# The front of an SSM and MLP kernel: a planner's order against a fixed list with idle products in it

## The chip, the cores and the metric

The kernel runs on one core of a Trainium2 chip. The metric is the device time of one execution, in microseconds (us). The kernel before takes 1021.8 us, the median of three runs (1018.9 to 1024.1). Five engines of the core work side by side, each through its own queue in order: TensorE (PE, matrix products, with its weight loads PEld), VectorE (DVE), ScalarE (ACT), GpSimd (POOL) and SyncE (SP), which starts most of the transfers.

## The reference: what is computed

`x` holds 2048 tokens of 640 channels. A vector `c` gives six rows of modulation, a shift, a scale and a gate for each half of the block:

```python
mod = (silu(c) @ w_mod).reshape(1, 6, 1, 640)
sa, ca, ga, sb, cb, gb = mod rows
h = layernorm(x) * (1 + ca) + sa
x = x + ga * S4(h)                # first half
h = layernorm(x) * (1 + cb) + sb
x = x + gb * (silu(h @ w1) * (h @ w3)) @ w2     # second half
```

`S4` convolves each channel over the 2048 tokens with a kernel of its own length. That convolution kernel is `K[d, l] = Re(sum over n of C B dt exp(dt A l))`, with 128 complex states `n` for each channel `d`; the reference convolves by Fourier transforms of twice the length, and adds `h * Dskip`.

## The kernel before, in words

The second half (the MLP, from about 430 us on) is not touched. The first half has these kinds of work, which the change and the prediction speak of by two-letter words:

- **Parameters** (`polar`, L221): from A, B, C and dt to the magnitudes and phases of every state. It runs once for the first 128 channels and once for the other 512. It uses logarithm and arctangent on ACT, and ends in four transposes on PE and in the split operands `lah`, `lal`, `lmh`, `lml`, from which exponentials are made.
- **Modulation** (`mod_early`, `mod_cols`, `mod_shift`, `mod_gate`, L278 to L344): `w_mod` is loaded in pieces of columns. A piece costs ten products of `silu(c)` with it, a copy to SBUF, and small products that turn the row into columns.
- **Token tiles**: 16 tiles of 128 tokens. Each is loaded (`ln1_load`), normed (`ln1_norm`), and sent through the first stage of the transform (`u_stage1`): products on PE, two copies out of PSUM, and a store to DRAM. Seven `x` tiles have room at a time.
- **Generation of the convolution kernel**: 40 steps of 16 channels. A step has phases on POOL (`PH`), absolute value, cosine and sine on ACT (`AB`, `CO`, `SI`), products for the exponents on PE and the exponentials on ACT (`PA`, `XA` and `PQ`, `XQ`), four table products on DVE (`E1`, `E2`, `A1`, `A2`), 64 small products on PE into the PSUM bank `pk` (`kg`), two operations on DVE that read `pk` (`K`), and a first transform stage (`pt` on PE, `uk` on ACT).
- **The convolution itself**: 40 steps, each with a transfer of twiddle factors, products (`st`), a copy (`kc`), products and sums on DVE (`T`, `Y`), inverse products with another transfer (`iv`), and a store (`zt`).

ACT holds one table of functions at a time: one for exponentials, one for sines, one for the logarithm, one for the arctangent. A change of table is an instruction of its own in ACT's queue.

The order is set in two ways. `keep` and `act` (L113 to L119) hold instructions in the order of the program text. Everything else is placed by a planner. Before, ACT is always held in order, and the other engines only once `in_order` is set. The front of the first half, from L702 to the end of the loop `for tk in range(LAG)` at L753, is planned: parameters, modulation and token tiles are written one after the other, with generation steps 0 to 9 in a loop, and the planner mixes them. After it comes a fixed list, `ROUND` (L805). It holds one pass over four generation steps and four convolution steps, in a fixed order on all engines, and is run ten times. What the front has already made is skipped, through the set `done`. So the first passes are short, and the third is the first with convolution steps in it.

Of the kernel before, what the change touches and what calls it, by code (L numbers as in the profile page):

```python
# [9 lines left out]
F32 = mybir.dt.float32  # L10
# [82 lines left out]
def tile_kernel(ctx: ExitStack, tc: tile.TileContext, a):  # L93
# [22 lines left out]

    def act(*args, **kw):

        return tc.keep_in_program_order(S.activation(*args, **kw))  # L119
# [26 lines left out]
    cT = kp.tile([P, KD], F32, name="cT")  # L146
    uk = kp.tile([P, 3, NA, DC], F32, name="uk")
# [18 lines left out]
    scb = pm_.tile([P, KD, NA], F32, name="scb")  # L166
# [3 lines left out]
    lt = pm_.tile([P, 2, D - DC], F32, name="lt")  # L170
    misc = pm_.tile([P, 9 * NA + 1 + P], F32, name="misc")
    selx, stepx = misc[:, :NA], misc[:, NA:4 * NA]
    s1r, c1, one4 = misc[:, 4 * NA:6 * NA], misc[:, 6 * NA:8 * NA], misc[:, 8 * NA:8 * NA + 1]
# [9 lines left out]
    def w_load(w, c0):  # L183

        n = w.shape[2]
        for i in range(c0 // 480, (c0 + n - 1) // 480 + 1):
            lo, hi = max(c0, i * 480), min(c0 + n, i * 480 + 480)
            nc.sync.dma_start(w[:, :, lo - c0:hi - c0], a["w_mod"][i][:, :, lo - i * 480:hi - i * 480])
        return w

# [23 lines left out]
    for t, n in ((misc, "misc"), (iota, "iota"), (ident, "ident")):  # L214
        nc.sync.dma_start(t, a[n])

    wm = [w_load(w, 256 * i) for i, w in enumerate(
        [w_room(1, 0, 256, 1280), w_room(1, 1, 256, 1280), w_room(1, 2, 256, 1280), w_table(), w_table()])]
# [57 lines left out]


    def mod_sums(w, pm):  # L278

        n = w.shape[2]  # L280
# [3 lines left out]
        part = pm_.tile([P, WC], F32, name="part", bufs=2)  # L284
        V.tensor_copy(part[:, :n], pm[:, :n])
        return part

    def mod_early(i, w, tag):

        pm = psS.tile([P, 512], F32, name="pm", tag=tag, bufs=1)  # L290
        n = w.shape[2]
        part = mod_sums(w, pm)
        for b in range(n // P):
            PE.matmul(pm[:, 256 + b:257 + b], part[:, b * P:(b + 1) * P], one4, start=True, stop=True)
        V.tensor_copy(cols.rearrange("p s k -> p (s k)")[:, 2 * i:2 * i + n // P], pm[:, 256:256 + n // P])

    def mod_shift():

        sa, ca, ga, zero, inv, r, gs = (cols[:, i] for i in range(7))
# [5 lines left out]

        pr = psS.tile([P, 2, 512], F32, name="pr", tag="Z", bufs=1).rearrange("p a b -> p (a b)")
        for k in range(KD):
            PE.matmul(pr[:64, k * P:(k + 1) * P], r[:, k:k + 1].broadcast_to([P, 64]), ident, start=True, stop=True)
        V.tensor_copy(rrow[:64], pr[:64, :D])
        rc = pm_.tile([P, WC], F32, name="part", bufs=2)[:, :KD * 2 * NA].rearrange("p (k c) -> p k c", k=KD)  # L310
        V.tensor_tensor(rc, bc(c1, 1, KD), bc(r, 2, 2 * NA), op=OP.mult)
        ps = psS.tile([P, 512], F32, name="ps", tag="pk", bufs=1)
# [6 lines left out]
        V.tensor_copy(shift, ps[:, :320])  # L319

    def mod_gate():

        V.tensor_tensor(cols[:, 6], cols[:, 1], cols[:, 2], op=OP.mult)
        gt = pm_.tile([P, WC], F32, name="part", bufs=2)[:, :KD * NA].rearrange("p (k g) -> p k g", k=KD)
        V.tensor_tensor(gt, bc(tog, 1, KD), bc(cols[:, 6], 2, NA), op=OP.mult)
        pg = psS.tile([P, 512], F32, name="pg", tag="pb", bufs=1)
        PE.matmul(pg[:, :KD * NA], toq, gt.rearrange("p k g -> p (k g)"), start=True, stop=True)
        V.tensor_copy(gaT, pg[:, :KD * NA])

    def mod_cols(i, w):  # L330

        pm = psS.tile([P, 2, 512], F32, name="pm", tag="Z", bufs=1)
        part = mod_sums(w, pm[:, 0])
        lo, hi = ((0, 3), (0, 3), (0, 3), (0, 1), (2, 3))[i]
        for b in range(lo, hi):
            PE.matmul(pm[:, 1, b:b + 1], part[:, b * P:(b + 1) * P], one4, start=True, stop=True)
        V.tensor_copy(modTf[:, 3 * i + lo:3 * i + hi], pm[:, 1, lo:hi])
        if i >= 3:

            row = part[:, P:] if i == 3 else part[:, :2 * P]  # L340
            PE.matmul(pm[:, 1, 256:], one4.broadcast_to([P, P]), row, start=True, stop=True)
            V.tensor_copy(gbr[:, (i - 3) * 256:(i - 3) * 256 + 256], pm[:, 1, 256:])
        if i == 4:
            V.tensor_scalar(modT[:, 1, :], modT[:, 1, :], 1.0, None, op0=OP.add)  # L344
# [3 lines left out]
    xt = [None] * NT  # L348

    def ln1_load(j):  # L350
        xt[j] = hpz.tile([P, D], F32, name="x", bufs=7)
        nc.sync.dma_start(xt[j], a["x"][j * P:(j + 1) * P, :])

    def ln1_norm(p):

        st = hpz.tile([P, 2, 2, 6], F32, name="st1")
        mv = hpz.tile([P, 2, 2], F32, name="mv1")
        rs = hpz.tile([P, 3, 2], F32, name="rs1")
        for i in range(2):
            for h in range(2):  # L360
                V.bn_stats(st[:, i, h, :], xt[2 * p + i][:, h * 320:h * 320 + 320])
            V.bn_aggr(mv[:, i, :], st[:, i])
        G.tensor_tensor(rs[:, 0, :], mv[:, :, 1], epst[:, 0:1].broadcast_to([P, 2]), op=OP.add)
        G.tensor_tensor(rs[:, 1, :], rs[:, 0, :], epst[:, 1:2].broadcast_to([P, 2]), op=OP.pow)
        V.scalar_tensor_tensor(rs[:, 2, :], mv[:, :, 0], -1.0, rs[:, 1, :], op0=OP.mult, op1=OP.mult)
        for i in range(2):
            x = xt[2 * p + i]
            act(x, x, AF.Identity, scale=rs[:, 1, i:i + 1], bias=rs[:, 2, i:i + 1])
# [4 lines left out]
    def u_stage1(j):  # L373
# [3 lines left out]
        u = hpz.tile([P, 4, D // 2], F32, name="u", bufs=2)  # L377
        pu = [psS.tile([P, 2, 512], F32, name="pu", tag=t, bufs=1) for t in ("Z", "AB"[j % 2])]
# [13 lines left out]
        if one:  # L392
            acopy(u[:, :2, :], pu[0][:, :, :320])
        else:
            V.tensor_tensor(u[:, :2, :], pu[0][:, :, :320], bc(shift, 1, 2), op=OP.add)
        V.tensor_tensor(u[:, 2:, :], pu[1][:, :, :320], bc(shift, 1, 2), op=OP.add)
        nc.sync.dma_start(usw[:, 4 * j:4 * j + 4, :], u)
# [21 lines left out]
    def exp_slow(steps):  # L419

        for s in steps:
            pQ[s] = psS.tile([P, 2, 512], F32, name="pq", tag="AB"[s % 2] if not in_order[0] else "B", bufs=1)
# [7 lines left out]

    def fast(s):

        AA[s] = a_table()
        act(AA[s][:, :, 0:3:2, :], pA.pop(s).rearrange("p r (j h b) -> p (r j) h b", j=8, h=2), AF.Exp)

    def slow(s):
        act(AA[s].rearrange("p (r j) s b -> p r j s b", r=2)[:, :, :, 1, :],
            pQ.pop(s)[:, :, :256].rearrange("p r (j b) -> p r j b", j=8), AF.Exp)

    def exps(s, between=()):  # L440

        steps = (s, s + 1)
        exp_fast(steps)
        for i in steps:
            fast(i)
        for fn in between:
            fn()
        exp_slow(steps)
        for i in steps:
            slow(i)  # L450

    def phases(s):
        sl = slice(s * SD, s * SD + SD)
        p = tp.tile([P, SD, NPH], I32, name="ph", bufs=4)
        hold = tc.keep_in_program_order if 0 < s < 4 else keep
        hold(G.tensor_tensor(p, bc(thi[:, sl], 2, NPH), bc(iota, 1, SD), op=OP.mult))  # L456
        keep(G.tensor_tensor(p[:, :, :NA], p[:, :, :NA], bc(phi[:, sl], 2, NA), op=OP.add))
# [14 lines left out]

    def trig(s):
        cosine(s)
        sine(s)
# [18 lines left out]

    def tables(s):
        for fn in (real1, real2, imag1, imag2):
            fn(s)
# [35 lines left out]
    def u_load(ch, i):  # L533

        fs = slice(i * 8, i * 8 + 8)
        for h in range(2):
            lo, hi = max(ch * DC, h * 320), min(ch * DC + DC, h * 320 + 320)
            if lo < hi:
                for c in range(2):
                    nc.sync.dma_start(uk[c * 64:c * 64 + 64, 0, fs, lo - ch * DC:hi - ch * DC],  # L540
                                      usr[h, c, :, fs, lo - h * 320:hi - h * 320])

    def stage2(ch, g):
        s2 = fp.tile([P, 4, P], F32, name="s2", bufs=3)
        nc.sync.dma_start(s2, a["s2"][:, g * 4:g * 4 + 4, :])
# [39 lines left out]
    def inverse1(ch, g):  # L585
        i1 = fp.tile([P, 2, 2, P], F32, name="i1", bufs=3)
        i1_last[0] = nc.sync.dma_start(i1, a["i1"][:, g * 2:g * 2 + 2])
        Y = Yq.pop((ch, g))
        if g % 2 == 0:
# [99 lines left out]
    conv = {"st": conv_part(stage2), "kc": conv_part(k_copy), "T": conv_part(products), "Y": conv_part(sums),  # L689
# [3 lines left out]
    def do(name, k):  # L693

        lo, hi = (LAG, LAG + 8 * NDC) if name in conv else (0, NS)
        if (name, k) in done or not lo <= k < hi or (name == "zt" and k % 2 == 0 and k < LAG + 8 * NDC - 8):
            return None
        done.add((name, k))
        return (conv if name in conv else parts)[name](k)

    act(sc, cT, AF.Exp, scale=-1.0)
# [4 lines left out]
    V.tensor_copy(scb, bc(sc, 2, NA))  # L706
# [5 lines left out]
    for j in range(4):  # L712
        ln1_load(j)
# [3 lines left out]
    do("PH", 0)  # L717
# [409 lines left out]
```

## Time and profile before

| | before |
|---|---|
| median of three runs | 1021.8 us |
| the profiled execution | 1021.7 us |
| its span, first to last instruction | 1019.8 us |
| mean granted PE clock | 0.953 |
| PE busy, DVE busy, ACT busy, POOL busy | 94%, 59%, 50%, 25% |
| up to 196.5 us: PE, DVE, ACT busy | 163.6, 140.0, 125.5 us |
| one full pass of ROUND | 28.4 us |

A row of a group of instructions gives its line, engine, operation and tiles, the count, then the busy time in us and the mean ns of one, then the idle time just before them and what ended it. A row of a timeline gives the start and the duration in us; a row of waits gives who waited for whom, the total, the times and the longest. The lines are shown where the prediction uses them.

### The profile page before, as it was taken

To read this page: it belongs to the slowest core of one execution; us is meant where nothing else is said; L and a number is where in the kernel's file an instruction comes from. 1 tells how busy PE (TensorE), PEld (TensorE's weight loads), DVE (VectorE), ACT (ScalarE), POOL (GpSimd) and SP (SyncE) were. 2 spreads that over 40 slices of the span, in tenths; PEclk is the share of its full clock that TensorE was granted. 3 is DMA by queue.
4 is the path that set the end of the run, shared out by engine and by line. 5 is a ranking of instruction groups with operands and counts; after the bars stand their busy time and mean duration, and the time that the engine had idled before them with its cause. 6 is when DMAs were issued, how large, how long until landed. Compare 5 with 4: busy or idle time off the path is not lost.

```text
span 1019.8 us, 20376 instructions
## 1 busy us (share of the span) xinstructions
PE 954.9 (94%) x8360; PEld 714.8 (70%) x8360; DVE 604.8 (59%) x1022; ACT 513.1 (50%) x699; POOL 254.3 (25%) x214
## 2 busy tenths in 40 slices
PE   5898797899899889899999999999999999999997
PEld 2544464666666666677788877788777788788886
DVE  4588966888888886664434555433645444533333
ACT  3658674999999954343234433334333344333321
POOL 1543332454454611221121111111111111111110
PEclk9955777999999999999999999999999999999999
DMA  9463495465555689686443454433533333433311
GB/s 273 154 229 121 179 212 178 127 166 134 142 148 151 177 209 269 203 228 158 120 117 98 134 178 136 123 98 95 179 96 102 91 91 93 148 95 99 96 39 52
DMA packets 107041, 146.31 MB, mean 143 GB/s; under 512 B 20836, under 2 KB 62948, under 8 KB 106948
## 3 DMA queue, kind: packets, MB, share of 16 engines
q1 hardware_dynamic: 104500, 140.09, 47.4%
q0 software_dynamic: 1024, 2.49, 0.9%
q10 hardware_dynamic: 1424, 2.43, 0.8%
q8 instruction: 66, 1.08, 0.4%
q14 instruction: 27, 0.22, 0.1%
HBM read 118.76 MB, written 26.21 MB: 142 GB/s over the span
## 4 chain that ended last, share of the span: by engine, by line
PE 71%; ACT 14%; DVE 7%; DMA 3%; POOL 2%; issue 2%; SPq 0%; DVEq 0%; ACTq 0%; POOLq 0%
PE acc L979 18%; PE pg L965 6%; PE pg L966 6%; PE pg L967 6%; PE pu L966 6%; PE pu L965 6%; PE pu L967 6%; ACT cs L119 3%; PE p L554 3%; ACT A L119 3%; ACT ph L119 3%; PE pa L416 2%; ACT L119 2%; PE pq L428 2%; PE pu L390 2%
## 5 line engine op out<-in xcount | busy, mean ns | idle before, releaser
L998 POOL TENSOR_TENSOR w<-w,gbr 128x512 f32<-128x512 f32 x55 | 83.6, 1520 | 399.6 <-DMA w<-in_w_dram 374.7
L456 POOL TENSOR_TENSOR ph<-thi,iota 128x1024 int32<-128x1024 int32 x40 | 85.4, 2136 | 176.7 <-DVE A L492 80.4
L965 PE MATMUL pg<-xh,gh 128*128 128x512 f32 x275 | 110.0, 400 | 0.1
L950 ACT CAST gh<-wg 128x640 fp32r<-128x640 f32 x55 | 40.2, 731 | 135.5 <-PE pg L966 129.2
L967 PE MATMUL pg<-xh,gl 128*128 128x512 f32 x275 | 107.5, 391 | 0.0
L966 PE MATMUL pg<-xl,gh 128*128 128x512 f32 x275 | 107.1, 389 | 0.0
L951 DVE TENSOR_TENSOR gl<-wg,gh 128x640 fp32r<-128x640 f32 x55 | 52.1, 948 | 89.4 <-ACT gh L950 86.5
L951 DVE TENSOR_TENSOR wl<-w,wh 128x640 fp32r<-128x640 f32 x55 | 47.7, 867 | 88.2 <-ACT wh L950 88.1
L965 PE MATMUL pu<-xh,uh 128*128 128x512 f32 x255 | 99.2, 389 | 0.0
L966 PE MATMUL pu<-xl,uh 128*128 128x512 f32 x255 | 99.2, 389 | 0.0
L967 PE MATMUL pu<-xh,ul 128*128 128x512 f32 x255 | 99.2, 389 | 0.0
L1023 DVE TENSOR_TENSOR hf<-pu,sg 128x512 f32<-128x512 f32 x52 | 36.0, 691 | 100.9 <-PE pu L967 100.9
L554 PE MATMUL p<-uk,s 128*64 128x256 f32 x640 | 79.3, 390 | 13.3 <-PE pa L416 5.6
L950 ACT CAST uh<-wu 128x640 fp32r<-128x640 f32 x51 | 37.3, 731 | 106.7 <-issue 67.8
L979 PE MATMUL acc<-wh,hh 128*128 128x512 f32 x224 | 87.6, 391 | 0.0
L979 PE MATMUL acc<-wl,hh 128*128 128x512 f32 x224 | 87.3, 390 | 0.0
L950 ACT CAST wh<-w 128x640 fp32r<-128x640 f32 x55 | 40.0, 727 | 91.1 <-PE acc L979 91.1
L979 PE MATMUL acc<-wh,hl 128*128 128x512 f32 x208 | 80.9, 389 | 0.0
L554 PEld LDWEIGHTS p<-uk,s 128*64 128x64 f32 x640 | 45.3, 138 | 39.0 <-PE pa L416 8.4
L965 PEld LDWEIGHTS pg<-xh,gh 128*128 128x128 f32 x275 | 51.6, 188 | 17.6 <-issue 5.6
L967 PEld LDWEIGHTS pg<-xh,gl 128*128 128x128 f32 x275 | 51.6, 188 | 11.3
L966 PEld LDWEIGHTS pg<-xl,gh 128*128 128x128 f32 x275 | 51.7, 188 | 10.1
(218 smaller groups left out, 2073.4 us busy)
## 6 DMA issues: line engine op xcount, KB each, us to landing
wg<-in_wg_dram SPq DMA_DIRECT2D x55, 320.0 KB
wu<-in_wu_dram SPq DMA_DIRECT2D x51, 320.0 KB
w<-in_w_dram SPq DMA_DIRECT2D x51, 320.0 KB
us<-u SPq DMA_DIRECT2D x16, 640.0 KB
s<-in_s_dram SPq DMA_DIRECT2D x40, 256.0 KB
i<-in_i_dram SPq DMA_DIRECT2D x40, 256.0 KB
uk<-us SPq DMA_DIRECT2D x32, 256.0 KB
zs<-zt SPq DMA_DIRECT2D x32, 256.0 KB
```

Of the source, the lines that this page charges most:

```text
L119: return tc.keep_in_program_order(S.activation(*args, **kw))
L390: PE.matmul(pu[h][hh * 64:hh * 64 + 64, q, :320], s1r[r], x[r, hh * 320:hh * 320 + 320], start=not (one and h == 0), stop=True, tile_posit ...
L456: hold(G.tensor_tensor(p, bc(thi[:, sl], 2, NPH), bc(iota, 1, SD), op=OP.mult))
L554: keep(PE.matmul(p2[par * 64:par * 64 + 64, pi, c, :], s2[:, pi * 2 + par, c * 64:c * 64 + 64], uk[:, 0:kn + 1:kn, f, :], start=True, stop ...
L950: S.copy(hi, src)
L951: V.tensor_tensor(lo, src, hi.bitcast(F32), op=OP.subtract)
L965: PE.matmul(ps, wh, xh, start=(i == 0), stop=False)
L966: PE.matmul(ps, wh, xl, start=False, stop=False)
L967: PE.matmul(ps, wl, xh, start=False, stop=(i == n - 1))
L979: PE.matmul(acc[k], lhs, rhs, start=(f == 0 and i == 0), stop=(f == NFT - 1 and i == len(terms) - 1))
L998: G.tensor_tensor(w2r[:, :512], w2r[:, :512], gbr, op=OP.mult)
L1023: V.tensor_tensor(hf, pu, sg, op=OP.mult)
```

## The change

The planned front and the first three passes of ROUND become one list, `FRONT`, of 572 words. All engines, SP too, follow it in its order. For that the functions are cut into small parts: one for the products of a modulation piece, one for its copy, one for its columns, and so on. The list ends with the words that end the third pass of ROUND (`A2+13`, `iv+13` and `SI+14` are the last of their kinds), and the remaining passes run as before.

77 of the words are `wm`: idle products of 128 by 512 on a tile, whose results nobody reads; the last digit of the word says how many. 140 such products stand in the list, and 40 more stand ahead of it, between parts of the first `polar`. They write to the bank `pk`, or to `Z` ahead of the list. The tile they read is the part of `lml` that the second `polar` fills later; until then it is set to zero.

Beside this:

- The second half of the modulation is loaded in eight pieces (seven of 256 columns and one of 128), not five of 384.
- The exponent products use one PSUM bank, `B`, throughout, and the first transform stage uses `Z` and `A` for every tile. Before, in the front, both alternated.
- The copy of `silu(c)` to 32 columns (`scb`, L706) is gone; the products read it with a repeated address.
- The twiddle loads have words of their own (`l2`, `l1`) ahead of their use.
- The loads of the first four token tiles for the second half are held behind the last inverse-matrix load.

```diff
+    V, G, PE = InOrder(nc.vector), InOrder(nc.gpsimd), InOrder(nc.tensor)
...
+    def load(out, in_):
+        ins = nc.sync.dma_start(out, in_)
+        return tc.keep_in_program_order(ins) if sp_order[0] else ins
...
+    PIECES = [(256 * i, 256) for i in range(7)] + [(1792, 128)] + [(1920 + 256 * i, 256) for i in range(7)] + [(3712, 128)]
...
-            PE.matmul(pm[g, :n], scb[:, k], w[:, k, :], start=(k < 4), stop=(k > 0), tile_position=(0, g.start))
+            PE.matmul(pm[g, :n], sc[:, k:k + 1].broadcast_to([P, NA]), w[:, k, :], start=(k < 4), stop=(k > 0),
+                      tile_position=(0, g.start))
...
-        pu = [psS.tile([P, 2, 512], F32, name="pu", tag=t, bufs=1) for t in ("Z", "AB"[j % 2])]
+        pu = puq[j] = [psS.tile([P, 2, 512], F32, name="pu", tag=t, bufs=1) for t in "ZA"]
...
-            pA[s] = psS.tile([P, 2, 512], F32, name="pa", tag="AB"[s % 2] if not in_order[0] else "B", bufs=1)
+            pA[s] = psS.tile([P, 2, 512], F32, name="pa", tag="B", bufs=1)
...
-        nc.sync.dma_start(xe[j], a["x"][j * P:(j + 1) * P, :])
+        with tc.issue_after(i1_last[0].ins):
+            nc.sync.dma_start(xe[j], a["x"][j * P:(j + 1) * P, :])
...
+    def warm(n, tag="pk"):
+
+        ps = psS.tile([P, 512] if tag == "pk" else [P, 2, 512], F32, name="ps", tag=tag, bufs=1)
+        ps = ps if tag == "pk" else ps[:, 0]
+        x = lml[:, 1:].rearrange("p k n -> p (k n)")
+        for _ in range(n):
+            PE.matmul(ps, x[:, :P], x, start=True, stop=True)
...
+    WARM = (25, 10, 5)
...
+    V.memset(lml[:, 1:].bitcast(F32), 0.0)
...
+    warm(WARM[0], "Z")
...
+    do("ms", 0)
+    warm(WARM[1], "Z")
...
+    do("ms", 1)
+    warm(WARM[2], "Z")
...
+    FRONT = (
+        "PA+0 PH+0 PH+1 XA+0 mc+0 mp+1 mc+1 mv+1 mv+0 lx+0 PQ+1 wm+1 ms+2 ms+3 XQ+1 AB+0 PQ+0 mp+2 PH+2 mc+2 mp+3 "
+        "mv+2 XQ+0 mc+3 ms+4 mv+3 wm+11 mp+4 PA+1 wm+21 mc+4 lb+0 lb+1 mv+4 lx+3 CO+0 wm+34 XA+1 AB+1 lx+2 sh+0 lb+2 "
...
+        "mp+5 ud+1 A2+0 lr+2 PA+2 mc+5 ln+3 mv+5 XA+2 lx+6 E2+1 v1+0 CO+3 g1+0 wm+72 PQ+3 ln+2 mp+6 XQ+3 lb+6 g2+0 "
...
+        "A1+13 pt+10 uk+10 wm+743 A2+13 st+14 AB+16 wm+753 iv+13 wm+765 SI+14 "
+    ).split()
+
+    in_order[0] = sp_order[0] = True
+    for word in FRONT:
+        do(*run(word))
+    sp_order[0] = False
...
-    for tk in range(LAG):
-        if tk == SPC + 1:
-            mod_cols(4, wm[4])
-            pre.close()
...
-        do("PH", tk + 3)
-        do("AB", tk + 2)
-        if tk % EB == EB - 2:
-            exps(tk + 2)
-            transform_k()
-            exps(tk + 4)
```

A word `name+k` calls part `name` for step `k`: `ms`, `mp`, `mc`, `mv` are the products, copy, columns and last copy of a modulation piece; `lw`, `lq`, `lg` its load; `lx`, `lb`, `lr`, `ls`, `ln` the load, statistics, deviation, mean and norm of a token tile; `up`, `ue`, `ud`, `us` its transform stage, its two copies and its store; `g1` to `g3`, `v1` to `v7`, `a1` to `a4` and `pT` the second `polar`, by engine; `lp` its load.

More of the change, by code (lines that the diff above doesn't have):

```diff
@@ L325, in mod_gate @@
         V.tensor_tensor(gt, bc(tog, 1, KD), bc(cols[:, 6], 2, NA), op=OP.mult)
[L326 to L344, printed above, removed]
+        pms["gt"] = gt
@@ L354, in ln1_norm @@
[L354 to L363, printed above, removed]
-        G.tensor_tensor(rs[:, 1, :], rs[:, 0, :], epst[:, 1:2].broadcast_to([P, 2]), op=OP.pow)
[L365 to L368, printed above, removed]
+        load(xt[j], a["x"][j * P:(j + 1) * P, :])
@@ L421, in exp_slow @@
         for s in steps:
-            pQ[s] = psS.tile([P, 2, 512], F32, name="pq", tag="AB"[s % 2] if not in_order[0] else "B", bufs=1)
+            pQ[s] = psS.tile([P, 2, 512], F32, name="pq", tag="B", bufs=1)
         for i, (w, rt) in enumerate(((lah, r1), (lal, r1), (lmh, None), (lml, None))):
@@ L698, in do, with close_first, run @@
         done.add((name, k))
+        if name in conv and fp is None:
+            fp = close_first()
         return (conv if name in conv else parts)[name](k)
+    def close_first():
+        assert not prt
+        pre.close()
+        pool = ssm.enter_context(tc.tile_pool(name="fp", bufs=2, side="right", reuse_waits="tile"))
+        if wm or pms:
+            late["part"] = pool.tile([P, D], F32, name="xe0", bufs=1)
+        return pool
+    def run(word, base=0):
+        name = word[:2].rstrip("+-")
+        return name, base + int(word[len(name):])
+    WARM = (25, 10, 5)
+    sp_order[0] = True
+    for word in "lw+0 lw+1 lw+3 lw+2 lx+1 lw+4".split():
+        do(*run(word))
+    sp_order[0] = False
     act(sc, cT, AF.Exp, scale=-1.0)
     act(dt, ldt, AF.Exp)
+    V.memset(lml[:, 1:].bitcast(F32), 0.0)
     V.tensor_scalar(sc, sc, 1.0, None, op0=OP.add)
@@ L805, in tile_kernel @@
+    FRONT = (
[30 rows of a table added]
+    ).split()
+    in_order[0] = sp_order[0] = True
+    for word in FRONT:
+        do(*run(word))
+    sp_order[0] = False
     ROUND = (
```

354 lines of the change are left out of this document (217 added, 137 removed), and 26 rows, old and new, of the table FRONT.

## The prediction

> **What bounds the kernel now.** I read the page first (span, engine shares, slices), then busy time by stretch, then the groups of instructions and the waits of the stretch that the change rewrites. The page:
>
> ```profile
> span 1019.8 us, 20376 instructions
> PE 954.9 (94%) x8360; PEld 714.8 (70%) x8360; DVE 604.8 (59%) x1022; ACT 513.1 (50%) x699; POOL 254.3 (25%) x214
> ...
> PE   5898797899899889899999999999999999999997
> ...
> DVE  4588966888888886664434555433645444533333
> ACT  3658674999999954343234433334333344333321
> ...
> PEclk9955777999999999999999999999999999999999
> ```
>
> A slice is 25.5 us. From the eighth slice on PE stands at eight or nine tenths and its clock at nine. Ahead of that, in the first 180 us, no engine is full and the granted clock is five to seven tenths. So the front is the one loose place, and the change is made there. By stretch (us from the span's start; busy time of each engine, then clock, DMA share, GB/s):
>
> ```profile
> core 0: us, PE busy (x) PEld busy (x) DVE busy (x) ACT busy (x) POOL busy (x), PEclk, DMA share, GB/s
> 0.00:18.00 18.00, 7.18 (x36) 2.82 (x36) 11.02 (x39) 8.52 (x16) 2.15 (x5) 1.00 0.94 274
> 60.00:121.70 61.70, 51.05 (x668) 28.25 (x672) 53.53 (x99) 45.27 (x56) 19.89 (x20) 0.58 0.55 198
> 121.70:196.50 74.80, 66.42 (x982) 42.06 (x968) 53.69 (x85) 52.65 (x63) 26.41 (x16) 0.80 0.64 168
> 225.00:253.40 28.40, 25.71 (x502) 18.98 (x500) 24.53 (x41) 26.39 (x33) 12.98 (x9) 1.00 0.51 135
> ...
> 0.00:196.50 196.50, 163.57 (x1894) 94.01 (x1896) 140.01 (x279) 125.51 (x156) 69.44 (x61) 0.77 0.61 187
> ```
>
> How long is the front? The new list ends with the last words of the third pass of ROUND: the fourteenth `A2` (L492) is its last work on DVE. In the trace that is the first row here; the other two are the ends of the next two passes:
>
> ```profile
> 195.79 0.68 DVE L492 SCALAR_TENSOR_TENSOR A<-ph,A 128x512 f32<-128x512 f32 x1
> ...
> 224.20 0.68 DVE L492 SCALAR_TENSOR_TENSOR A<-ph,A 128x512 f32<-128x512 f32 x1
> ...
> 252.57 0.68 DVE L492 SCALAR_TENSOR_TENSOR A<-ph,A 128x512 f32<-128x512 f32 x1
> ```
>
> The front now takes 195.79 + 0.61 (to the start of the next pass) = 196.4 us. A pass takes 28.4 us, in which ACT is busy 26.39, or 0.929: with a fixed list ACT can be kept that full, beside PE at 0.905 and DVE at 0.864. In the front as it is ACT has 125.5 of 196.5 us. What it waits for there:
>
> ```profile
> ACT A L119 <- PE pa L416: 17.8, 6, 9.2
> ACT x L119 <- DVE rs L365: 10.4, 3, 5.7
> ACT A L119 <- PE pq L428: 9.4, 9, 4.7
> ACT u L122 <- PE pu L390: 9.0, 2, 7.3
> ACT kc L122 <- PE p L554: 8.6, 1, 8.6
> ACT uk L122 <- PE pt L523: 5.3, 2, 3.3
> ```
>
> 50 us of PE's products and 10 us of DVE's norms: order and PE's slow clock, not lack of work. What follows the front is the same program in both kernels, at clock 1.0, with PE full, so a shorter front should be a shorter run, microsecond for microsecond.
>
> **The change part by part.**
>
> *ACT's work in the new order.* Each change between exponentials, sines, logarithm and arctangent reloads ACT's table:
>
> ```profile
> L119 ACT ACT_TABLE_LOAD x13 | 16.7, 1283 | 1.4 <-PEq L1116 1.2
> ...
> 187.76 1.28 ACT L119 ACT_TABLE_LOAD   x1
> 189.06 1.15 ACT L119 ACTIVATE cs<-cs,hp 128x1024 f32<-128x1024 f32 x1
> ```
>
> The front has 13 loads now. In the new list I count the places where an `XA`/`XQ` word (exponential) follows a `CO`/`SI` word (sine), or the reverse, or `a2`, `a3` come between: 31, and three stand ahead of the list (Exp, Ln, Arctan). 34 less 13 is 21 more, by 1.283 us: 26.9 us. All else on ACT is the same work in another order. So ACT's front costs 125.5 + 26.9 = 152.4 us. The bounds of a switch are 1.28 (the load alone) and, hidden in a wait, nothing; I take the whole, as ACT is to be the fullest engine.
>
> The Trainium skill (ScalarE: Activation LUTs, What ACT_TABLE_LOAD costs) gives a switch about 1283 ns for the load and some 1380 ns more for a drain. By it the 21 switches would cost 29 us more than I take, 31 us at ACT's share of 0.929, and the forecast would be about 1030 us. The rows above disagree with the second part: the load ends at 189.04 and the next activation starts at 189.06.
>
> *The start.* The first exponential ends a chain through DVE and PE:
>
> ```profile
> 14.71 1.28 ACT L119 ACT_TABLE_LOAD   x1
> 25.18 1.02 ACT L119 ACTIVATE A<-pa 128x1024 f32<-128x1024 f32 x1 [9.18 <-PE pa L416]
> ...
> 16.46 0.28 DVE L270 TENSOR_TENSOR lal<-pT,lah 128x128 fp32r<-128x128 f32 x1
> ...
> 171.04 0.50 PE L416 MATMUL pa<-r,lah 32*128 32x512 f32 x2
> 171.37 0.40 PE L416 MATMUL pa<-r,lal 32*128 32x512 f32 x2
> ```
>
> Its last operand is ready at 16.74, but its four products are mixed among modulation products until 25. In the list they come first (`PA+0`). Four such products take 0.73 us at the full clock (171.04 to 171.77) and twice that at half; with the way over the semaphores ACT starts at about 18.5, 6.7 us sooner. ACT's work up to there is 8.5 us, so 152.4 - 8.5 = 143.9 remain.
>
> *PE and the idle products.* A low clock lengthens every product, and idle products cost time too:
>
> ```profile
> L416 PE MATMUL pa<-r,lah 32*128 32x512 f32 x4 | 2.4, 789 | 0.0
> ...
> L416 PE MATMUL pa<-r,lah 32*128 32x512 f32 x22 | 5.5, 495 | 0.0
> ...
> 417.34 5.50 PE L870 MATMUL ps<-idle 128*128 128x512 f32 x16 [0.73 <-issue]
> ...
> PE pk L505 <- DVE K L513: 0.6, 1, 0.6
> ```
>
> The first row is from the first 30 us, the second from 175 to 250. (The page's clock of nine in the first two slices isn't borne out by the first row, which is the slow rate; I go by the row.) The ratio is 0.63, and PE's 163.6 us of the front ran partly fast already, so I estimate 0.7 of it, 115 us, with 103 (0.63) and 164 (nothing gained) as ends. The change adds 40 idle products ahead of the list and, by the last digits of its 77 `wm` words, 140 in it: 180. The only idle products in the trace, 16 in 5.50 us, cost 0.34 us each across a change of the clock; by the ratio above about 0.24 at the full one: 43 us, at most 62. PE then has 158 us in the new front, 0.91 of 173 us, as full as in the passes (0.905). It is no looser than ACT, but it does not set the sum, unless the clock stays low.
>
> Will the clock hold? In the passes PE at 0.905 keeps 1.0; between 60 and 121.7 us, at 0.83, it got 0.58. So 0.91 should hold it, with little to spare. The Trainium skill (TensorE: Matmul & The Clock Gate, Part 1) has the array throttled until one window of about 3.4 us was busy, and again after one idle window; by that, any group of idle products in each gap is enough. The trace is sterner: 0.58 with PE busy 51 of 62 us.
>
> *DVE and POOL.* DVE loses a copy of 160 columns (L706) and gains a memset and four small copies from cutting the second half of the modulation into eight pieces and not five: under 1 us either way. 140 us less 11 up to 18 us leaves 129 of some 155 us, 0.83, under the passes' 0.864. POOL has 69.4 us, 0.4. Both are hidden by ACT; if ACT were faster, DVE would be next, at 18 + 129/0.864 = 167 us.
>
> *SP and the loads.* The same bytes go through SP; its 0.61 share of the DMA engines becomes 0.69. The `x` loads (L352) waited 49.1 us in all on SP for tiles to come free, with modulation loads and stores of `u` behind them:
>
> ```profile
> SPq L352 <- PE pu L390: 49.1, 8, 18.6
> ```
>
> In the list the first seven take free tiles, and `lx+7` stands behind `up+1`, which frees its tile; stores `us` stand behind their `ue` and `ud`. I cost this at nothing, with -3 to +6 us as bounds (the first parameter load took 5.7 us; the second, `lp`, now comes later). The single bank for `pa` and `pq` makes a step's two exponentials a chain of 0.9 + 1.0 + 1.2 + 0.6 us with their waits, 16 times about 4.5 = 72 us, hidden under 155. The loads of the first four token tiles for the second half move behind the last inverse-matrix load; they are used some 20 us later; nothing.
>
> *The sum.* ACT's 143.9 us at the 0.929 that a fixed list reaches in the passes take 154.9 us; from 18.5 the front ends at 173.4 and not 196.4: 23.0 us less. The profiled execution took 1021.7 us (1019.8 of span and 1.9 around it; the median of the runs is 1021.8), so **999 us**. With ACT never idle the front ends at 162.4: 988 us. With ACT at 0.85, worse than the passes, at 187.8: 1013 us.
>
> **The rivals.**
>
> 1. *Idle products tie PE to DVE* (slower). They write the bank `pk`, which `kgen` fills and DVE's `K` reads. On PE, in order, an idle product waits for that read, and the real products queue behind it; PE waits, so the exponentials wait. For it: 77 groups, and DVE in strict order as well, so that one late operation holds the rest. Against: only 0.6 us of such a wait in the front so far, and the list puts each group behind its `K`. It eats the 23.0 us if a group holds ACT up by 0.30 us on average; at 0.5 us the front grows by 77 x 0.5 - 23 = 15.5 us: 1037 us. In ACT's share, the point is 143.9/177.9 = 0.81; from 60 to 196.5 us it has 0.72 now.
>
> 2. *The clock stays low part of the way.* At 0.83 busy it fell. If half of the front ran at half rate, PE would have 79 + 79/0.63 = 204 us, at 0.905 an end at about 227 and 1052 us. Against: 0.91, and idle products put in the gaps.
>
> 3. *The order brings little*: the table loads eat what it saves, ACT stays at 0.81, about 1022 us. For it: 34 loads where 13 did.
>
> 4. *ACT and PE without gaps*: 988 us or a little less.
>
> 5. *The drain at each switch*, by the page's rule: ACT stands 1.38 us longer 21 times, 29/0.929 = 31 us, about 1030 us; the row at 189.06 speaks against it.
>
> **How the numbers follow.** The forecast, 986 to 1013 us, has 0.69; the even faster case below that 0.04; the first rival 0.13, the second 0.05, the third 0.07, the fifth 0.02. That gives faster by over 0.5% (below 1016.7; what the runs shown, 1018.9 to 1024.1, can tell from no change) 0.73, within it 0.07, slower 0.20. The range runs from 986 into the slower cases, to 1028, which leaves about 0.04 below and 0.16 above.
>
> **What the profile after would show.** Right: the fourteenth `A2` on DVE (its line will differ) ends at 162 to 188 us; ACT has about 34 table loads in the front, is busy about 152 us there and at nine tenths after 20 us; the first `A<-pa` starts before 20 us; the clock is at nine tenths from the second slice on; the passes after it still take 28.4 us. Wrong: long waits of PE's idle products for DVE's `K`, of ACT for `pa` and `pq`, clock figures of five in the front, or SP waiting in front of an `lg` or `lp` load with POOL and DVE idle behind.

## The result and the profile after

The changed kernel takes 1036.2 us in the median of four runs (1031.4 to 1046.5), the kernel before 1022.9 us: 1.0138 times as long, with a 95% interval of 1.0096 to 1.0181. The forecast was 999 us. The profiled execution is the longest of the four. The four differ in how long PE's clock was low: 1046.5, 1036.6, 1035.8 and 1031.4 us go with a mean granted clock of 0.959, 0.968, 0.971 and 0.975.

The page of the changed kernel, same parts as before:

```profile
span 1044.6 us, 20822 instructions
PE 987.5 (95%) x8570; PEld 738.4 (71%) x8570; DVE 617.5 (59%) x1027; ACT 542.0 (52%) x720; POOL 257.9 (25%) x214
...
PE   8779999978889988899999999999999999999997
...
DVE  4785778758888887755444364444555534533332
ACT  4972788869999993343334433334433344333331
...
PEclk8765799999999999999999999999999999999999
```

PE is fuller at the start than it was, and the clock is still five to eight tenths in the first five slices (a slice is now 26.1 us). By stretch, the columns as in the prediction:

```profile
18.00:60.00 42.00, 35.94 (x239) 20.73 (x243) 27.62 (x66) 34.81 (x37) 22.55 (x20) 0.68 0.47 155
60.00:121.70 61.70, 56.20 (x550) 31.35 (x535) 41.43 (x75) 33.20 (x41) 14.12 (x16) 0.58 0.36 130
121.70:209.20 87.50, 82.90 (x1235) 51.78 (x1231) 69.93 (x109) 75.14 (x82) 34.91 (x20) 1.00 0.60 165
209.20:230.00 20.80, 15.27 (x236) 10.01 (x234) 9.28 (x16) 11.67 (x15) 5.72 (x3) 0.92 0.55 147
248.40:276.80 28.40, 25.69 (x502) 18.99 (x500) 24.50 (x41) 26.38 (x33) 12.98 (x8) 1.00 0.54 145
```

And the last `A2` of the list, and the one after it, on DVE (all instructions that are held in order now carry the line of a helper, L125, and transfers L131, so they are told apart by their tiles):

```profile
208.60 0.69 DVE L125 SCALAR_TENSOR_TENSOR A<-ph,A 128x512 f32<-128x512 f32 x1
...
227.31 0.69 DVE L125 SCALAR_TENSOR_TENSOR A<-ph,A 128x512 f32<-128x512 f32 x1
```

This splits the 24.8 us by which the span of the profiled execution is longer. The list ends at 208.6 us where the front ended at 195.8: 12.8 us. From there to the next `A2` it takes 18.7 us, where it took 7.4 (203.2 after 195.8): 11.3 us. The full passes after that take 28.4 us as before. The last 0.7 us is spread over the rest.

The second loss has its place in SP's queue and in PE's wait. SP's longest wait and what SP starts around it, then PE's wait:

```profile
SPq L765 <- ACT uk L139: 21.4, 1, 21.4
...
203.54 1.14 SPq L765 DMA_DIRECT2D zs<-zt  x2
204.78 3.21 SPq L131 DMA_DIRECT2D uk<-us  x4
208.03 0.62 SPq L131 DMA_DIRECT2D s<-in_s_dram  x1
...
209.17 0.90 SPq L131 DMA_DIRECT2D s<-in_s_dram  x2
```

```profile
214.32 3.44 PE L125 MATMUL p<-uk,s 128*64 128x256 f32 x16 [4.70 <-DMA s<-in_s_dram]
```

SP, now in strict order, stood 21.4 us at the store of the first inverse steps (`zt`), and the loads for the fifth convolution step stood behind it.

The first loss is PE's. Below are what DVE does ahead of PE's longest wait in the list, that wait, and the stretch that follows:

```profile
68.59 3.35 DVE L125 RECIPROCAL uk<-uk 128x512 f32<-128x512 f32 x1
...
74.28 0.81 PE L125 MATMUL pu<-rrow,misc 1*64 1x320 f32 x4 [4.60 <-DVE u L125]
...
74.00:118.40 44.40, 43.95 (x407) 23.86 (x411) 24.80 (x50) 19.41 (x23) 11.18 (x14) 0.50 0.34 127
```

PE waits from 69.7 to 74.3 us, because DVE does a reciprocal of 3.35 us ahead of the copies PE needs. The clock falls to half at 74.0 and stays there for 44.4 us, though PE is busy 43.95 us of them. DVE and ACT are half idle beside it. That it stays low so long is not fixed by the program: experiment 3 has the same gap, and a short spell after it.

### The profile page after: what moved, and what is told of

Its sections match the earlier page's. It is cut to its first block, busy times and chain, and to the rows that moved or that the text cites. A ratio compares the mean times of both kernels' runs of the same rounds, so it can differ in the third digit from the quotient of the medians.

```text
span 1044.6 us, 20822 instructions
## 1 busy us (share of the span) xinstructions
PE 987.5 (95%) x8570; PEld 738.4 (71%) x8570; DVE 617.5 (59%) x1027; ACT 542.0 (52%) x720; POOL 257.9 (25%) x214
## 4 chain that ended last, share of the span: by engine, by line
PE 75%; ACT 11%; DVE 6%; DMA 4%; issue 2%; POOL 1%; SPq 1%; ACTq 0%; DVEq 0%
PE pu L125 19%; PE pg L125 19%; PE acc L125 17%; PE ps L125 6%; PE p L125 4%; ACT cs L136 3%; ACT A L136 2%; PE pa L125 2%; PE pq L125 2%; PE pk L125 2%; PE pt L125 2%; ACT ph L136 2%; ACT L136 2%; PE pz L125 2%; DVE uk L125 2%
## 5 line engine op out<-in xcount | busy, mean ns | idle before, releaser
L125 POOL TENSOR_TENSOR w<-w,gbr 128x512 f32<-128x512 f32 x55 | 82.8, 1505 | 398.4 <-DMA w<-in_w_dram 388.4
L125 POOL TENSOR_TENSOR ph<-thi,iota 128x1024 int32<-128x1024 int32 x40 | 86.5, 2162 | 176.7 <-DVE A L125 132.6
L125 PE MATMUL pg<-xh,gh 128*128 128x512 f32 x280 | 112.3, 401 | 0.1
L125 PE MATMUL pg<-xh,gl 128*128 128x512 f32 x280 | 109.4, 391 | 0.0
L125 PE MATMUL pg<-xl,gh 128*128 128x512 f32 x280 | 109.0, 389 | 0.0
L125 DVE TENSOR_TENSOR gl<-wg,gh 128x640 fp32r<-128x640 f32 x55 | 51.5, 936 | 88.7 <-ACT gh L1117 87.9
L125 PE MATMUL pu<-xh,uh 128*128 128x512 f32 x260 | 101.2, 389 | 0.0
L125 PE MATMUL pu<-xh,ul 128*128 128x512 f32 x260 | 101.1, 389 | 0.0
L125 PE MATMUL pu<-xl,uh 128*128 128x512 f32 x260 | 101.1, 389 | 0.0
L125 DVE TENSOR_TENSOR wl<-w,wh 128x640 fp32r<-128x640 f32 x55 | 48.1, 874 | 88.3 <-ACT wh L1117 88.2
L125 PE MATMUL p<-uk,s 128*64 128x256 f32 x640 | 79.8, 391 | 19.1 <-DMA s<-in_s_dram 6.7
L125 DVE TENSOR_TENSOR hf<-pu,sg 128x512 f32<-128x512 f32 x52 | 36.0, 692 | 99.9 <-PE pu L125 99.9
L1117 ACT CAST uh<-wu 128x640 fp32r<-128x640 f32 x51 | 37.3, 731 | 106.7 <-issue 67.7
L125 PE MATMUL acc<-wh,hh 128*128 128x512 f32 x224 | 87.6, 391 | 0.0
L125 PE MATMUL acc<-wl,hh 128*128 128x512 f32 x224 | 87.3, 390 | 0.0
L125 PE MATMUL acc<-wh,hl 128*128 128x512 f32 x208 | 80.9, 389 | 0.0
L125 DVE TENSOR_TENSOR E<-A,cs 128x1024 f32<-128x1024 f32 (+1 forms) x80 | 79.2, 1015 | 0.0
L125 PE MATMUL ps<-lml 128*128 128x512 f32 x180 | 75.2, 515 | 3.9 <-DVE lml L125 1.7
L125 PEld LDWEIGHTS p<-uk,s 128*64 128x64 f32 x640 | 45.1, 139 | 45.2 <-issue 10.8
L125 PEld LDWEIGHTS pg<-xh,gh 128*128 128x128 f32 x280 | 52.6, 188 | 18.7 <-issue 6.0
```

Source lines behind the costliest of these rows:

```text
L125: return lambda *args, **kw: keep(fn(*args, **kw))
L1117: S.copy(hi, src)
```

## The experiments

Thirteen kernels; "list end" is the start of the fourteenth `A2` in the profiled execution, "low" the time at half clock in its first 230 us by the trace's clock record. That record says 1.0 until its first entry, whatever the rows show. With idle products ahead of the list the first entry comes by 8 us; without them (before, 1 and 7) it comes at 41 to 46 us, so their "low" is too small by 23 us or more, as shown under 1. Each ratio is against runs of the kernel before on the same chip, whose medians lay between 1020.9 and 1022.9 us.

| kernel | median us | ratio to before | list end | low |
|---|---|---|---|---|
| before | 1022.9 | 1 | 195.8 | 92 |
| the change | 1036.2 | 1.0138 (1.0096 to 1.0181) | 208.6 | 82 |
| 1 no idle products | 1030.6 | 1.0078 (1.0055 to 1.0102) | 190.7 | 85 |
| 2 idle products ahead of the list only | 1028.3 | 1.0062 (1.0038 to 1.0086) | 189.9 | 99 |
| 3 loads ahead of the store | 1026.2 | 1.0050 (1.0018 to 1.0081) | 192.8 | 44 |
| 4 gap filled | 1029.9 | 1.0077 (1.0045 to 1.0108) | 190.0 | 44 |
| 5 both mends (3 and 4) | 1023.3 | 1.0010 (0.9983 to 1.0036) | 192.6 | 41 |
| 6 both, no sine tables | 1016.4 | 0.9948 (0.9925 to 0.9970) | 188.1 | 31 |
| 7 loads ahead, no idle products | 1021.6 | 1.0000 (0.9980 to 1.0020) | 194.6 | 85 |
| 8 both, x loads back | 1022.6 | 1.0011 (0.9991 to 1.0031) | 190.2 | 38 |
| 9 both, idle in the first half only | 1017.5 | 0.9964 (0.9943 to 0.9986) | 189.9 | 65 |
| 10 both, idle groups doubled | 1047.4 | 1.0271 (1.0219 to 1.0324) | 210.9 | 27 |
| 11 both, one product per group | 1024.9 | 1.0047 (1.0028 to 1.0067) | 197.4 | 68 |
| 12 as 9, no sine tables | 1018.9 | 0.9979 (0.9959 to 1.0000) | 184.9 | 55 |
| 13 as 9, a second gap filled | 1021.7 | 1.0008 (0.9993 to 1.0023) | 189.5 | 58 |

### 1 and 2: without idle products

```diff
     def warm(n, tag="pk"):
+        return
```

> The changed kernel without any of its 180 idle products (40 ahead of the list, 140 in it); nothing else is changed. In the profiled execution of the change they take 75 us of PE's 189 us up to 209 us, mostly at the low clock. Theory A (the idle products are a load: PE is full with them and the clock stays low all the same): the front is shorter without them, 1010 us or less. Theory B (they hold the clock in the stretches where it is high; without them it is low for longer, and the clock is what counts): 1030 us or more, with the first 120 us at half rate nearly throughout.

The second keeps the calls ahead of the list and drops the words:

```diff
-"wm": lambda k: warm(k % 10)
+"wm": lambda k: None
```

> The changed kernel with the 40 idle products ahead of the list and without the 140 in it. Theory A (load): near the kernel without any, 1010 us or less, the 40 stand where PE has nothing else to do. Theory B (clock): between 1025 and 1040 us, as the clock drops at the first gap, by 20 us, and comes back late. If it is well below the kernel without any, the 40 ahead are worth having by themselves.

1030.6 and 1028.3 us: not the 1010 of a mere load. Both lie in theory B's ranges, but they are not the loss against the change that B is about. Without any idle products the clock is low for longer, as B says: 85 us by the record, and also from the first exponent products to the record's first entry at 41.3 us. These products take 0.79 us there, the slow rate:

```profile
17.94 0.79 PE L125 MATMUL pa<-r,lah 32*128 32x512 f32 x2 [1.27 <-DVE lml L125]
...
30.38 0.79 PE L125 MATMUL pa<-r,lah 32*128 32x512 f32 x2
```

All the same the lists end at 190.7 and 189.9, 18 us sooner than in the profiled change and 2 to 3 us sooner than in experiment 3, whose clock held. The next `A2` comes at 208.6 in the first, still 17.9 us later, so the second loss does not come from the idle products. The 180 idle products bought no time. Whether the 5.6 us without them are a gain is not clear: the intervals of the two ratios overlap.

### 3: the loads ahead of the store

```diff
-kg+12 zt+11 Y+12 st+13 ul+2 ... wm+721 l2+14 iv+12 ... wm+731 l1+13
+kg+12 ul+2 l2+14 l1+13 zt+11 Y+12 st+13 ... wm+721 iv+12 ... wm+731
```

> The changed kernel with three load words (the third u load, the transfers of the fifth convolution step) moved in SP's order from behind the store of the first two inverse steps to ahead of it. In the profile of the change SP stands 21 us at that store, and PE then stands 4.7 us at the fifth step's products, whose transfer starts at 209 us. Theory: this is what makes the first pass after the list 11 us longer, and 8 to 11 us come back (about 1026 us). Rival: PE is late there for its own reasons (the sums, the banks), and it changes by under 3 us.

1026.2 us, 10 us less, the theory's figure. The transfer for the fifth step starts before the list ends, and PE no longer waits for it there (last `A2` of the list, and the next; then SP):

```profile
192.81 0.69 DVE L125 SCALAR_TENSOR_TENSOR A<-ph,A 128x512 f32<-128x512 f32 x1
...
205.24 0.69 DVE L125 SCALAR_TENSOR_TENSOR A<-ph,A 128x512 f32<-128x512 f32 x1
...
187.74 1.13 SPq L765 DMA_DIRECT2D zs<-zt  x2
188.97 1.76 SPq L131 DMA_DIRECT2D uk<-us  x2
190.78 0.70 SPq L131 DMA_DIRECT2D s<-in_s_dram  x1
```

12.4 us between the two, where the change has 18.7 and the kernel before 7.4: 6.3 of the 11.3 us come back here. Of the 10 us in the medians, the rest can't be put down to this edit: this profile also had its clock low for 38 us less, after the same gap. The gap, the stretch after it, and the thirteenth `A2`, which stands in the list ahead of the moved words, here and then in the change:

```profile
74.02 0.81 PE L125 MATMUL pu<-rrow,misc 1*64 1x320 f32 x4 [4.60 <-DVE u L125]
...
74.00:118.40 44.40, 42.39 (x587) 25.18 (x587) 37.09 (x73) 31.21 (x39) 14.94 (x16) 0.89 0.56 194
...
182.95 0.68 DVE L125 SCALAR_TENSOR_TENSOR A<-ph,A 128x512 f32<-128x512 f32 x1
```

```profile
198.75 0.68 DVE L125 SCALAR_TENSOR_TENSOR A<-ph,A 128x512 f32<-128x512 f32 x1
```

Up to that place both run the same words, and one execution is 15.8 us ahead of the other. So the first loss is that of an execution with a long low spell, not of every execution of the change. Nine of this kernel's ten runs have a mean clock of 0.971 to 0.977 and take 1024.1 to 1029.1 us; the tenth has 0.958 and takes 1039.3 us.

### 4: the gap filled

```diff
-"a3+0 us+0 ue+3 gp+0 PH+5
+"a3+0 us+0 ue+3 gp+0 wb+18 PH+5
...
+"wb": lambda k: warm(k, "B")
```

> The changed kernel with 18 more idle products, in the bank of the exponents, at the place where PE stands 4.6 us (69.7 to 74.3 us) for copies behind a reciprocal on DVE. They take about 4.3 us at the full clock. Theory C (this one gap drops the clock for the 44 us that follow, and the clock sets the time there): the granted clock stays at 1.0 well past 74 us and the time falls by 8 to 18 us, to 1018 to 1028. Rival D (the small products and groups of one to five idle ones don't hold the clock either; it falls soon after by itself): within 4 us of the change, with the clock down by 85 us.

The same stretch as above:

```profile
74.00:118.40 44.40, 42.05 (x590) 24.88 (x591) 38.59 (x74) 32.94 (x40) 15.36 (x18) 0.92 0.56 200
```

The clock is 0.92 and not 0.50, and in the same 44.4 us PE does 590 products for 407, DVE 38.6 us of work for 24.8. The list ends at 190.0 and not 208.6. But this doesn't show theory C: in experiment 3 the gap was left open, and the same stretch looks much the same (0.89, 587 products). In the medians it is 6.3 us, just outside the range expected. The change's other runs had less low clock than its profile, so there was less to win, and how much of the 6.3 us is the filling's is not shown.

### 5: both mends

> The changed kernel with both mends: the three load words ahead of the store, and 18 idle products in the 4.6 us gap. If the two losses stand side by side, the gains add up (10 and 6 us against the change): about 1020 us, the level of the kernel before. Rival: the gap only moves work from before to behind the list's end, and it stays at the 1026 us of the loads alone.

1023.3 us, level with the kernel before. It lies between the two expectations. With the clock low for only 41 us and no load late at its end, the list still ends at 192.6 us. So even then the list itself saves 3 us, not 23.

### 6: table loads

```diff
-act(cs[s], cs[s], AF.Sin, ...)
+act(cs[s], cs[s], AF.Identity if sp_order[0] else AF.Sin, ...)
```

The same is done for the sine.

> The kernel with both mends, and in the list the sines and cosines are computed as an identity, which needs no table of its own, so the loads for changes between exponentials and sines are gone from the list (about 27 of 34; some 35 us of ACT); this leaves the true sines of the first steps out and changes nothing else. Theory E (the added table loads are what keeps the list from being shorter, since ACT stands in every step's chain): the list ends 15 to 25 us sooner than with both mends alone, about 1000 us in all. Rival F (PE with its idle products, and DVE in strict order, set the time; ACT has room for the loads): under 5 us.

Eight table loads are left in the first 190 us, of 33. ACT loses 32 us of work and the list ends 4.5 us sooner (the median is 6.9 us lower). That is nearer to F than to E: ACT had room. The clock was up a little longer too (low for 31 us, not 41), so the loads' own share may be smaller still. What has none, from 140 to 190 us:

```profile
140.00:190.00 50.00, 49.87 (x692) 31.90 (x688) 42.24 (x63) 30.70 (x38) 20.15 (x11) 1.00 0.76 176
```

### 7 and 8: idle products, x loads

The seventh kernel has the edits of 1 and 3.

> The changed kernel with the three load words ahead and without any idle products. Without idle products alone it was 1030.6 us. If idle products are worth about nothing on the whole and the loads are worth 8 to 10 us whatever else is there: about 1021 us. If the idle products help only once the loads no longer hold PE up (at the list's end the clock was low without them): 1024 to 1028 us.

1021.6 us: the gain of the loads adds to that of leaving the idle products out (9.0 against 10.0 us alone). By the record the clock is low twice as long as with both mends, in fact longer still (the first entry comes at 40.6 us), and the time is the same.

```diff
-        with tc.issue_after(i1_last[0].ins):
-            nc.sync.dma_start(xe[j], ...)
+        nc.sync.dma_start(xe[j], ...)
```

> The kernel with both mends and with the loads of the first four token tiles of the second half where they were before, not held behind the last inverse-matrix load. In the profiles the stretch from the 38th step's last table product to the first product of the MLP's output is 84.5 us before and 85.6 to 86.9 in the kernels with the change. If the x loads do that, 1 to 2 us come back; rival: it is another cause (the order of the last convolution steps' stores), and the time is that of both mends within 1 us.

Within 0.6 us of both mends: the rival. Where the `x` loads stand makes no difference that can be measured.

### 9 to 11: is PE the bound?

```diff
-"wm": lambda k: warm(k % 10)
+"wm": lambda k: warm(k % 10) if k < 250 else None     # 9
+"wm": lambda k: warm(2 * (k % 10))                    # 10
+"wm": lambda k: warm(1)                               # 11
```

> The kernel with both mends and without the idle groups of the list's second half (the last 52 of 77, from about 125 us on); the 40 ahead, the first 25 groups and the 18 in the gap stay. A lone idle product holds PE 0.42 us at the full clock (from its start to the next product's), each further one 0.235, so PE is relieved of some 28 us of the 176 it is busy up to the list's end. Theory G (PE with its idle products is what sets the list's length: 176 us at the 0.905 of the passes is 194 us, measured 192.6): the list ends 10 to 20 us sooner if the clock holds there as it does in the passes after it; 1005 to 1013 us. Rival H (without them the clock falls in that half, as it did without any): 1019 to 1025 us.

> The kernel with both mends and each idle group of the list doubled: 140 more products of 0.235 us, 33 us more on PE, a little less where the clock is now low and then holds. Theory G (PE is full in the list): the list ends 25 to 36 us later, 1045 to 1060 us. Rival I (the groups stand in gaps, in which PE would wait anyway): under 10 us more.

> The kernel with both mends and one product in each of the 77 idle groups: 63 fewer, 15 us less on PE. Theory G: the list ends 8 to 15 us sooner, 1008 to 1015 us, if one product per group holds the clock. Rival H: the clock is low for longer and the time is within 3 us of both mends (1023 us).

Doubling is the clearest. The groups of idle products up to the list's end, of both mends and of the doubled kernel, then the last `A2` of each list in the same order:

```profile
L125 PE MATMUL ps<-lml 128*128 128x512 f32 x188 | 72.2, 484 | 4.8 <-DVE K L125 2.2 <-DVE lml L125 1.7 <-DVE cols L125 1.0
...
192.62 0.68 DVE L125 SCALAR_TENSOR_TENSOR A<-ph,A 128x512 f32<-128x512 f32 x1
```

```profile
L125 PE MATMUL ps<-lml 128*128 128x512 f32 x317 | 102.1, 448 | 2.1 <-DVE lml L125 1.7 <-DVE cols L125 0.3 <-DVE K L125 0.2
...
210.91 0.69 DVE L125 SCALAR_TENSOR_TENSOR A<-ph,A 128x512 f32<-128x512 f32 x1
```

30 us more of idle products end the list 18.3 us later and cost 24.1 us in the median: most of an added idle product's time is time of the kernel. The list's end moves by less than the 25 to 36 us expected of a full engine, so some do stand in gaps. Taking the second half's groups away (9) gains 5.8 us in the median, between the ranges of G and H. In the profile the list ends only 2.7 us sooner, and the rest comes just behind it (9.1 us to the next `A2`, not 12.4). The clock does fall there, to 0.86 from 140 to 190 us, as H said. That may have cost what the idle products did; no run separates the two:

```profile
140.00:190.00 50.00, 42.08 (x644) 28.28 (x646) 39.42 (x61) 43.14 (x48) 18.89 (x10) 0.86 0.68 153
```

One product per group (11) has the worst of both: the clock is low for 68 us and the list 4.7 us longer than with both mends; 1024.9 us, as H said.

### 12 and 13: what is next

The twelfth is 9 with the edit of 6; the thirteenth puts ten idle products into the gap at 37 us.

> Both mends, idle groups in the list's first half alone, and identities in place of the list's sines and cosines (the true sines of the first steps are left out), so that some 25 table loads, 32 us of ACT, are gone. With all idle products on PE this was worth 7 us. Theory J (with PE relieved, ACT with its added loads is next: it is busy 0.86 of 140 to 190 us): 12 to 25 us under the kernel with idle groups in the first half, 993 to 1005 us. Rival K (the chain of PE, DVE and ACT through single banks sets the time, table loads or not): 4 to 8 us, about 1011 us.

> Both mends, idle groups in the list's first half alone, and ten more idle products (2.5 us) in the gap of 36.8 to 39.2 us, where PE waits for an exponential; after it the clock was low for 27 us in every profile with idle products. If that gap alone drops the clock, it stays at 1.0 until 60 us or later, and the list ends 3 to 8 us sooner, about 1012 us. Rival: the groups after it are too thin, the clock falls at the next gap (44.9 us), and the time stays at 1017 us.

Without the sine tables the list ends 5.0 us sooner in the profile, and the median is not lower (1018.9 against 1017.5, ratios whose intervals overlap). ACT's added loads are not what holds the time once PE is relieved either; K is nearer, though its 4 to 8 us did not come. The filled gap keeps the clock up for seven more microseconds, to 45.8, in the next gap (43.3 to 46.6 us, PE waiting for an exponential): the rival. But the time is 1021.7 us and not 1017, with an interval apart from that of 9. In the profile the list ends 0.5 us sooner than in 9, and 4.1 us are lost behind its next `A2`, where the two programs are the same; the cause is open.

## Why the prediction was wrong

**The front and the passes after it.** Right: the full passes still take 28.4 us, with 25.69, 24.50 and 26.38 us of PE, DVE and ACT in them, and what changed lies ahead of them. The start was right too: the first exponential starts at 19.3 us for 18.5 expected.

**ACT's work.** The term was right: 47 table loads in the whole run where there were 26, so 21 more; ACT is busy 8.5 + 34.8 + 33.2 + 75.1 = 151.7 us up to 209 us, for 152.4 forecast.

**ACT's share.** This is the step that failed: "ACT's 143.9 us at the 0.929 that a fixed list reaches in the passes". Measured is 143.1 us in 191.2, 0.75, in the change's profile, and 0.83 in the kernel with the gap filled (142.4 of 172), whose clock held. At 0.83 the sum gives 18.5 + 143.9/0.83 = 191.9 us and not 173.4, and where the clock held (3, 4, 5 and 8) the list ends at 190.0 to 192.8. The point from which it decides was put at 0.81. The share of the passes was carried over to a stretch with another bound. ACT was not the engine whose work set the length: 25 fewer table loads, 32 us, moved the list's end by 4.5 us.

**PE and the idle products.** PE's row was written out and then set aside as "no looser than ACT, but it does not set the sum, unless the clock stays low". Of it the products that compute something were right: some 117 us (189.2 less 71.9 of idle products) for 115. Two things were off. First, a lone idle product was costed at the price of one in a row, 0.24 us. Of the 77 groups, most hold one or two. A lone one holds PE 0.43 us at the full clock, 0.73 at the low one, from its start to the next product's:

```profile
200.24 0.49 PE L125 MATMUL ps<-lml 128*128 128x512 f32 x1
200.67 1.09 PE L125 MATMUL pt<-s,K 128*64 128x128 f32 x16
...
82.94 0.80 PE L125 MATMUL ps<-lml 128*128 128x512 f32 x1
83.67 1.98 PE L125 MATMUL pt<-s,K 128*64 128x128 f32 x16
```

Summed that way over the trace, and without the waits, the 140 in the list hold PE 57.7 us in the change and an estimated 47 at the full clock, for 34 (140 x 0.24) by the price taken. Second, the clock. "In the passes PE at 0.905 keeps 1.0 ... so 0.91 should hold it" was refuted by the same window as in the profile before: from 60 to 121.7 us PE is busy 56.2 us, 0.91, and the clock is 0.58 again. PE's 189.2 us up to 209.2 (14.13 + 35.94 + 56.20 + 82.90) are 0.904 of it, the share of the passes, where ACT has 0.73. That makes PE the fullest engine of that list, and experiment 10 shows that more work on it lengthens the list. It doesn't show that PE alone sets the length: without idle products (1) PE is busy 143.8 of 190.7 us, 0.75, and the list ends there all the same.

**SP at nothing, -3 to +6 us.** Wrong: 11.3 us at the list's end, of which 6.3 went with three words moved. The term was taken from the `x` loads and the `u` stores, and not from the end of the list, where a store waits for ACT and the next step's transfers are queued behind it.

**DVE and POOL.** No run shows either to be the bound. But "under 1 us either way" was wrong for DVE: up to the list's end it is busy 150.5 us, where the front had 140.0, and 12.7 us more in the whole run (617.5 for 604.8), spread over many operations. And a DVE operation in strict order, the reciprocal, held PE up for 4.6 us, after which the clock was low for 44 us in that execution and for 6.8 in experiment 3's.

**The rivals.** The first (idle products wait for `K`) was to decide from 0.30 us a group, 23 us in all. In the change's front there is this much of it (2.2 us with both mends):

```profile
PE ps L125 <- DVE K L125: 1.2, 1, 1.2
```

That wait didn't happen, and that its 1037 us lies next to the measured 1036 is luck. What it said beside it, that one late operation of DVE in strict order holds the rest, did happen once, at the reciprocal. The second, a clock that stays low part of the way, happened in the profiled execution, and had 0.05: its sum was 204 us of PE, an end at 227 and 1052 us; PE has 189 us, the end is 209, and that run took 1046.5. It is not the whole: without idle products the clock was low for longer still, and the list ended at 190.7. The third (table loads eat the saving) gave a time nearer than the forecast, by luck, for a reason that experiment 6 does not bear out. The drain of the fifth is nowhere in the changed kernel's rows: up to 210 us, after 28 of the 34 loads the next activation starts 0.01 to 0.02 us after the load's end.

**Left open.** The list was to end at 173.4 us. Of the 35 us to the 208.6 of the profile, 15.8 are those between its execution and experiment 3's. Of the 19 us that remain with the clock up, leaving out the sine tables and the second half's idle products (12) takes 7.7 us, from 192.6 to 184.9. The other 11.5 us are open. With the loads ahead and PE relieved (9 and 12), no engine is over 0.87 from 140 to 190 us and the list still ends at 185 to 190. Single banks (`B` for both exponents, `Z` and `A` for the token tiles) and DVE's strict order are candidates; neither was tried. DVE itself is nearly as full as in the passes there: in 12 it is busy 140.7 us of the 166.9 from 18 us to the list's end, 0.84, for 0.864. Nor is it settled why the clock came back at 118.4 and not sooner.

## What to carry to other kernels

Work out every engine's row for the new program to its end, with the price of a product in the place where it stands, before choosing which row sets the sum; an engine that is "about as full" can be the bound as soon as one of its prices is off. A share reached in one stretch is not a price for another. Idle work on an engine that is nearly full costs most of what it takes there: 18 of 30 us here, with PE at 0.92 before. A group of one costs nearly twice the product in a row. Before a loss seen in one profile is put down to the program, the same stretch is to be compared in a second execution. A queue put into strict order needs its waits read one by one: here three words that were moved gave back twice what the list saves (6.3 us in the profile, for 3). The kernel with both mends and idle groups only in the first half is a little faster than both kernels: 1017.5 us, 0.9964 of before (0.9943 to 0.9986).

## What the runs showed of the hardware

A busy PE is not enough to raise the clock: between 74.0 and 118.4 us it was busy 43.95 of 44.4 us and the granted clock was 0.50 throughout. Most products there use 32 rows or 32 columns of the array, in between groups of one to five full idle products. The 25 full ones in a row at the start had raised it within 4 us of their start (1.7 to 5.8 us; they start 0.43 us apart before, 0.23 after). The Trainium skill (TensorE: Matmul & The Clock Gate, Part 1) has the gate open after one busy window of about 3.4 us; for such mixtures this trace disagrees, with thirteen windows of that length in a row. In experiment 3 the same words brought it back at 80.0 us, 6.8 us after it fell, so the mixture alone does not decide it; what does is open.

It falls after short gaps: those of 2.4 us (37.3 to 39.7) and 1.6 us (16.9 to 18.5) were each followed by the low clock within a microsecond (at 39.9 and 19.4), and with ten products in the first of them (13) the clock stayed up to 45.8. How long it is low differs from run to run of the same program: the four runs of the change spread over 15 us, with mean clocks from 0.959 to 0.975.
